# Retention attention with a routed expert layer on one core: loads in halves, and the first and last steps in another order

## The chip, the cores and the metric

The kernel runs on one core of one Trainium2 chip. A core has five engines that run their own instruction lists beside each other: TensorE (PE, matmuls), VectorE (DVE), ScalarE (ACT), GpSimd (POOL) and SyncE (SP, which here issues most of the transfers between memory and the core). They wait for each other only by semaphores. The core's 16 DMA engines move the data. The metric is device time in microseconds (us) of the core, from launch to end; lower is better.

## The reference

Attention here is a retention recurrence without softmax: per head a state of 64 x 64 decays by gamma and takes in k v^T, and the query reads it. Its result, 3072 tokens of 512 features, goes to a layer of 4 groups of 4 experts; each token takes the best group and in it the best expert, and its row is scaled by the product of both softmax weights.

```python
# q, k, v: (4, 8, 768, 64)   batch, heads, tokens, head size
gamma = 1 - 2 ** (-5 - arange(8));  scale = 1 / sqrt(64)
for t in range(768):
    state = gamma * state + k[:, :, t] (x) v[:, :, t]
    y[:, :, t] = scale * q[:, :, t] @ state
x = y as (3072, 512)
g = argmax(x @ w_group);  e = argmax(x @ w_expert[g])
out[token] = g_weight * e_weight * relu(x @ w1[g, e]) @ w2[g, e]   # 512 -> 1024 -> 512
```

## The kernel before

**Attention.** The 768 tokens of a sequence are 6 chunks of 128. A step takes one chunk of two sequences, so there are 12 steps (NS2 = 12; step i is chunk i % 6). A chunk is computed with full matrices: scores of its own 128 tokens (`score_mm`), masked to the lower triangle on DVE (`score_mask`, pf), times the values (`value_out`), plus the state of the chunks before times the queries (`state_out`), both added in PSUM (op). The values are scaled beforehand by a power of gamma on POOL (`vprep`, vs). `keys_mm` transposes the keys on PE and ACT copies them (kk); `state_mm` adds kk x vs to the state, and ACT copies it (V). `out_x` multiplies op by the decay table gx on DVE: xt, the step's output. One step later xt gives the router's logits (`logits_mm`, ACT copies them to ls) and is transposed to rows of tokens (`trans_mm`, ACT copies them to xr), which SP writes to the scratch tensor xd; four small matmuls in `trans_mm` (L326, the selections) bring the logits to a token per partition in the bank log.

**Routing.** Per two steps one batch of 512 tokens is routed (`route`): on DVE max, exp (ACT), group and expert hits (oh, L374); on PE the ranks of the tokens within their experts (L399, L401); on DVE the slot numbers (slot, L419) and the weights (six small operations, L382 to L394, which end in src). POOL then scatters (token, weight) by slot into the lists `meta` in memory, four scatters per batch (`enlist`, L440).

**Experts.** Experts 0 and 1 are computed in two parts: ua, va with the tokens of the first 12 chunks, which start while attention still runs, and ub, vb with the rest. The 14 others follow in order of their counts, as us[0] to us[13] (`order` sorts on DVE). An expert needs its weights (wf, four tiles of 1 MB, which SP loads), split into a high half in f16 (wh, ACT, L616) and a low half in bf16 (wl = wf - wh, DVE, L618); its list (mt, SP, L630) and the rows of its tokens by an indirect gather on POOL (xg, L640); their transposes (tpx, PE) split into xbh (ACT) and xbl (DVE, L661). A product is three matmuls of halves: hps = xbh wh + xbl wh + xbh wl (L681), its positive part goes to hh (ACT) and hl (DVE, L689), and the second product yps follows alike (L713). The result is weighted on ACT and scattered by POOL to the output (L814).

**Order.** No scheduler sets it: each engine runs its instructions in the order in which the Python code writes them. `attention` writes the steps; its callback `beside(i, place)` puts the early experts' work between them, and `extra` the early splits on POOL and ACT. `run` then writes the passage to the experts by hand: `first(n)` takes n half pieces of ua's first product, of which there are eight, and `route` is a generator that gives way at "wait" and "ranks". `self.held` collects the hl operations of this passage, to be written later.

**Banks.** PSUM has eight banks: sh0 to sh2 (tag "big", also the hidden products), sh3 (tag "tra"), op (two, "mid"), log, and "sta" (state, later free). The scores of the first sequence go to sh0 and sh1, of the second to sh2 and sh3; logits, transposes and key transposes share them. Who writes a bank next waits for its last reader.

**Transfers.** SP issues the loads in the order of the code: at the start first q, k of step 0 by halves, the constants `cst` (571 columns, 285.5 KB) between them, then the other loads of steps 0 to 2 and the decay table. A q, k or v of a step is one transfer of 128 x 1024 (512 KB), and so is kt for two steps and the write of xr.

## Time and profile before

| | us |
|---|---|
| median of three runs | 427.3 (426.33 to 429.1) |
| the profiled execution, its own time | 427.34 |
| its span in the trace | 425.6 |
| PE busy | 404.0 (95%) |
| DVE busy | 290.1 (68%) |
| ACT busy | 222.8 (52%) |
| POOL busy | 175.9 (41%) |

Times within the trace count from the start of the span. Attention fills the first 107 us, the passage to the experts ends near 135 us, and the experts take the rest. A row of the timeline gives the start, the length, the engine, the line, what is written and read, and in brackets how long the engine had been idle before and what ended that. Rows that follow each other are put together (x32); of such a row the bracket is that of the first. PE's matmuls are pipelined, so a row's length holds the end of its last matmul, and the next row can start within it. The profile's granted clock is a share of full speed, 2.4 GHz.

### The profile page before, as it was taken

The numbers are of one execution on the slowest core, as the hardware profiler recorded it, in microseconds if no ns is written. First come the engines' busy times: TensorE is split into PE (matmuls) and PEld (weight loads), VectorE is DVE, ScalarE is ACT, GpSimd is POOL, SyncE is SP. The second block draws the span as 40 slices with busy tenths as digits, with TensorE's granted clock in tenths as the row PEclk, the third lists the DMA queues.
The fourth block names the chain that finished last, engine by engine and source line by source line (L and its number), as shares of the span: only waits on it lengthen the run. The fifth ranks groups of instructions, "written<-read, shape, count | busy, mean of one in ns | idle before, by whom it ended". The sixth has DMA issues, their size and how long they took to land.

```text
span 425.6 us, 13495 instructions
## 1 busy us (share of the span) xinstructions
PE 404.0 (95%) x5692; PEld 332.4 (78%) x5721; DVE 290.1 (68%) x473; ACT 222.8 (52%) x342; POOL 175.9 (41%) x153
## 2 busy tenths in 40 slices
PE   8899999999798999999999999999999999999991
PEld 4789888787675768585979788897978878879791
DVE  4455585578892557776889786867768777787620
ACT  2135336446541556646556665665766657667520
POOL 4445669748877022340508142351513405222001
PEclk9999999999999999999999999999999999999996
DMA  8999999997536867776776786978788797896001
GB/s 282 378 313 327 373 306 339 336 285 243 161 94 236 333 220 249 245 258 235 257 246 214 259 277 239 315 246 283 266 286 284 272 306 270 280 327 233 27 9 34
DMA packets 36913, 107.94 MB, mean 254 GB/s; under 512 B 13784, under 2 KB 13784, under 8 KB 29684
## 3 DMA queue, kind: packets, MB, share of 16 engines
q1 hardware_dynamic: 25908, 89.76, 61.9%
q0 software_dynamic: 10944, 17.31, 11.7%
q8 instruction: 45, 0.74, 0.7%
q14 instruction: 16, 0.13, 0.1%
HBM read 94.65 MB, written 13.77 MB: 255 GB/s over the span
## 4 chain that ended last, share of the span: by engine, by line
PE 58%; issue 26%; POOL 6%; DMA 4%; DVE 2%; SPq 1%; ACT 0%; POOLq 0%; DVEq 0%; ACTq 0%
PE hps L681 19%; PE yps L713 8%; PE yps L759 6%; PE yps L761 5%; PE op L291 5%; POOL out L814 4%; PE sh L227 3%; POOL xg L640 2%; PE op L278 2%; DMA gx<-dec 2%; PE sh L322 2%; PE tpx L658 2%; PE stp L253 2%; PE sh L310 2%; PE sh L212 1%
## 5 line engine op out<-in xcount | busy, mean ns | idle before, releaser
L618 DVE TENSOR_TENSOR wl<-wf,wh 128x1024 bf16<-128x1024 f32 x120 | 148.5, 1248 | 40.0 <-ACT wh L616 35.4
L681 PE MATMUL hps<-xbh,wh 128*128 128x128 f16 (+14 forms) x576 | 134.2, 245 | 0.9 <-ACT xr L329 0.9
L681 PE MATMUL hps<-xbl,wh 128*128 128x128 bf16 (+14 forms) x576 | 134.2, 245 | 0.3 <-issue 0.3
L616 ACT ACTIVATE wh<-wf 128x1024 f16<-128x1024 f32 (+1 forms) x136 | 133.5, 1002 | 1.8 <-DMA wf<-w1p 1.8
L681 PE MATMUL hps<-xbh,wl 128*128 128x128 f16 (+14 forms) x576 | 134.2, 245 | 0.1
L814 POOL DMA_INDIRECT out<-yo,mt x32 | 41.3, 1289 | 180.4 <-ACT yo L796 152.7
L681 PEld LDWEIGHTS <-wh 128*128 128x128 f16 x1152 | 102.5, 98 | 4.7 <-issue 1.9
L640 POOL DMA_INDIRECT xg<-xd,mt x32 | 52.5, 1641 | 26.3 <-DMA mt<-meta 17.4
L686 ACT ACTIVATE hh<-hps 128x256 f16<-128x256 f32 (+14 forms) x72 | 35.1, 488 | 52.3 <-PE hps L681 51.5
L761 PEld LDWEIGHTS <-wh 128*128 128x128 f16 x704 | 44.7, 98 | 21.0
L681 PEld LDWEIGHTS <-wl 128*128 128x128 bf16 x576 | 56.3, 98 | 1.1 <-issue 0.5
L239 DVE TENSOR_TENSOR pf<-sh,cst 128x512 f32<-128x512 f32 x48 | 30.8, 685 | 30.0 <-PE sh L227 10.3
L689 DVE SCALAR_TENSOR_TENSOR hl<-hps,hh 128x256 bf16<-128x256 f32 (+14 forms) x69 | 38.1, 553 | 16.7 <-ACT hh L686 14.2
L660 ACT ACTIVATE xbh<-tpx 128x512 f16<-128x512 f32 (+13 forms) x32 | 16.9, 527 | 47.2 <-PE tpx L658 47.1
L661 DVE TENSOR_TENSOR xbl<-tpx,xbh 128x512 bf16<-128x512 f32 (+13 forms) x32 | 19.2, 601 | 21.5 <-ACT xbh L660 21.5
L440 POOL DMA_INDIRECT meta<-src,slot x24 | 27.6, 1151 | 14.3 <-DVE src L394 7.1
L759 PE MATMUL yps<-wh,hh 128*128 128x512 f16 x88 | 33.4, 380 | 0.0
L759 PE MATMUL yps<-wh,hl 128*128 128x512 f16 x88 | 33.4, 379 | 0.0
L187 POOL TENSOR_TENSOR vs<-lv,cst 128x512 f32<-128x512 f32 x24 | 24.6, 1047 | 20.8 <-DMA lv<-qkv 10.9
L761 PEld LDWEIGHTS <-wl 128*128 128x128 bf16 x352 | 23.1, 98 | 10.4
L761 PE MATMUL yps<-hh,wl 128*128 128x103 f16 (+10 forms) x352 | 26.3, 197 | 1.2
L761 PE MATMUL yps<-hl,wh 128*128 128x103 bf16 (+10 forms) x352 | 26.3, 197 | 0.0
(146 smaller groups left out, 600.0 us busy)
## 6 DMA issues: line engine op xcount, KB each, us to landing
wf<-w1p SPq DMA_DIRECT2D x26, 1024.0 KB
wf<-w2p SPq DMA_DIRECT2D x26, 1024.0 KB
xd<-xr SPq DMA_DIRECT2D x12, 512.0 KB
lq<-qkv SPq DMA_DIRECT2D x11, 512.0 KB
lk<-qkv SPq DMA_DIRECT2D x11, 512.0 KB
lv<-qkv SPq DMA_DIRECT2D x11, 512.0 KB
wf<-w1p SPq DMA_DIRECT2D x16, 256.0 KB
wf<-w2p SPq DMA_DIRECT2D x16, 256.0 KB
```

What stands on the lines that cost most here:

```text
L239: nc.vector.tensor_tensor(o, sc, tri, ALU.mult)
L440: i = nc.gpsimd.indirect_dma_start(out=self.metaf, out_offset=bass.IndirectOffsetOnAxis(ap=slot[:, c:c + 1], axis=0), in_=src[:, c, :], in ...
L616: nc.scalar.activation(u["wh"][i][:, cs], u["wf"][i][:, cs], AF.Copy)
L618: (eng or nc.vector).tensor_tensor(u["wl"][i][:, cs], u["wf"][i][:, cs], u["wh"][i][:, cs], ALU.subtract)
L640: nc.gpsimd.indirect_dma_start(out=xg[0:r, i, :], out_offset=None, in_=self.xd[0:n, :], in_offset=bass.IndirectOffsetOnAxis(ap=mt[0:r, i, ...
L681: nc.tensor.matmul(hv[:, a, 0:W], l[:, k, fs], r[:, k, 0:W], start=(n == 0), stop=(n == 11))
L686: nc.scalar.activation(hh[:, f, 0:W], hv[:, :, 0:W], AF.Relu)
L689: nc.vector.scalar_tensor_tensor(*rest)
L713: nc.tensor.matmul(ps[0:r, :], l[:, k, ts], m[k], start=(n == 0), stop=(n == 23))
L759: nc.tensor.matmul(big, h[:, k, 0:P], w[k], start=(n == 0), stop=(n == 23))
L761: nc.tensor.matmul(yv[:, d, 0:r], w[k][:, d * P:d * P + P], h[:, k, P:P + r], start=(n == 0 and d == 0), stop=(n == 23), skip_group_check= ...
L814: s = nc.gpsimd.indirect_dma_start(out=self.out, out_offset=bass.IndirectOffsetOnAxis(ap=mt[0:r, i, 0:1].bitcast(U32), axis=0), in_=yo[0:r ...
```

## The change

It has eight parts, none of which alters what is computed.

1. Loads of q, k, v, kt and the writes of xr go in two transfers of 256 KB each.
2. The constants are two tiles: `cst` (308 columns, 154 KB, what the first steps use) keeps its place, `rest` (263 columns) comes last in the front's order. That order puts the decay table ahead of v1, q2 and k2. The cast of `stri` moves to the end of step 1.
3. In steps 0 and 1 the scores of the next step are written behind `out_x` (in step 1 they stood around `state_out`), so xt stands ahead of the masks. The key transposes of steps 1 and 2 use log and sh0.
4. Selections of steps 4, 8, 9 and 10 are postponed into the next step (`late`, `select_late`).
5. In the last two batches the weights are written directly behind the hits, not behind the slots.
6. The low splits (wl) of va move behind the slots, the held hl and xbl of va; the high splits (wh) are dealt anew over the last step and the passage. `xlow(ua)` stands behind the last xt.
7. The last step's logits have a bank of their own (tag "sta"), its xr a buffer of its own; the fourth hidden product of ua and va uses "tra", the other three "big". The transposes of the last step stand ahead of all hidden products. ACT clears the buffer xg1 in place of POOL.
8. The gathers of ub and vb stand directly behind the last scatters on POOL. At step 10 POOL's scaling `vprep` stands ahead of the gathers of ua and va. Two in place of four weight parts go ahead of the early lists on SP.

Here is SP's row of transfers at the start, in the kernel before (lq, lk, lv are the loads, a number more is another tile, gx the decay table):

```order
L122 DMA cst_93<-cst 128x571
L177 DMA lq_94<-qkv 128x512
L177 DMA lk_96<-qkv 128x512
L177 DMA lv_150<-qkv 128x512 x2
L177 DMA lq_153<-qkv 128x1024
L177 DMA lk_155<-qkv 128x1024
L177 DMA lq_157<-qkv 128x1024
L177 DMA lk_159<-qkv 128x1024
L177 DMA lv_161<-qkv 128x1024
L190 DMA gx_116<-dec 128x512
L879 DMA wr_114<-wr 128x4x20
```

And with the change:

```order
L125 DMA cst_93<-cst 128x308
L179 DMA lq_95<-qkv 128x512
L179 DMA lk_97<-qkv 128x512
L179 DMA lv_150<-qkv 128x512 x2
L179 DMA lq_153<-qkv 128x512 x2
L179 DMA lk_156<-qkv 128x512 x2
L192 DMA gx_117<-dec 128x512
L179 DMA lv_160<-qkv 128x512 x2
L179 DMA lq_163<-qkv 128x512 x2
L179 DMA lk_166<-qkv 128x512 x2
L908 DMA wr_115<-wr 128x4x20
L906 DMA rest_94<-cst 128x263
```

The decay table stands three loads of a whole step further ahead, and the tile of the constants ahead of the second q and k is smaller.

DVE in the last step and the passage, before, from the hits of the fifth batch (oh) to the first row of the sixth:

```order
L374 TENSOR_TENSOR oh<-log,go 128x64
L661 TENSOR_TENSOR xbl<-tpx,xbh 128x4x128
L303 TENSOR_TENSOR xt<-op,gx 128x512 x2
L407 TENSOR_TENSOR log<-log,nb 128x64
L410 TENSOR_TENSOR nb<-log,nb 128x16
...
L419 CAST slot<-log 128x4
L382 TENSOR_REDUCE log<-ex 128x20
...
L394 RECIPROCAL src_127<-log 128x4
L618 TENSOR_TENSOR wl<-wf,wh 128x1024 x3
L689 SCALAR_TENSOR_TENSOR hl<-hps,hh 128x2x128
L358 TENSOR_REDUCE m<-log 128x20
```

With the change, the same stretch:

```order
L391 TENSOR_TENSOR oh<-log,go 128x64
L399 TENSOR_REDUCE log<-ex 128x20
...
L411 RECIPROCAL src_127<-log 128x4
L306 TENSOR_TENSOR xt<-op,gx 128x512 x2
L687 TENSOR_TENSOR xbl<-tpx,xbh 128x4x128
L426 TENSOR_TENSOR log<-log,nb 128x64
...
L438 CAST slot<-log 128x4
L375 TENSOR_REDUCE m<-log 128x20
```

and further on, behind the sixth batch's slots, where the splits now stand:

```order
L438 CAST slot<-log 128x4
L449 TENSOR_SCALAR rows_2187<-nb 1x1
L449 TENSOR_SCALAR rows_2189<-nb 1x1
L1117 SCALAR_TENSOR_TENSOR hl<-hps,hh 128x2x128 x4
L687 TENSOR_TENSOR xbl<-tpx,xbh 128x4x128
L637 TENSOR_TENSOR wl<-wf,wh 128x1024 x4
L480 TENSOR_TENSOR cnt<-nb,rest 1x16
```

The weights have moved ahead of the last xt, and three splits that stood between the fifth batch's weights and the sixth batch's hits now stand, with a fourth, behind the sixth batch's slots and ahead of the list that `order` makes.

POOL in the passage, before, from the last early split to the gathers of ub and vb:

```order
L618 TENSOR_TENSOR wl<-wf,wh 128x512
L1054 MEMSET xg_1973 128x1024
L440 DMA meta<-src_129,slot 57600x2 x4
L594 TENSOR_LOAD ord
L814 DMA out<-yo,mt 3072x512
L640 DMA xg_80<-xd,mt 128x512 x2
L590 ISA
```

With the change:

```order
L637 TENSOR_TENSOR wl<-wf,wh 128x512
L459 DMA meta<-src_129,slot 57600x2 x4
L659 DMA xg_80<-xd,mt 128x512 x2
L613 TENSOR_LOAD ord
L841 DMA out<-yo,mt 3072x512
L609 ISA
```

The clearing is gone from POOL, and the two gathers stand ahead of the read of the sorted order and of ua's output.

The diff, cut to its core:

```diff
@@ load
-        n, f = "qkv".index(name), slice(us[0] * DM, us[-1] * DM + DM)
-        self.nc.sync.dma_start(st[name].rearrange("p u f -> p (u f)")[:, f], self.a_qkv[n, i][:, f])
+        for u in us:
+            self.nc.sync.dma_start(st[name][:, u], self.a_qkv["qkv".index(name), i][:, u * DM:u * DM + DM])
@@ logits_mm
-        lt = self.sh[bank][:, 0:2 * P]
+        lt = self.pp.tile([P, 512], F32, name="lgt", tag="sta", bufs=1) if bank is None else self.sh[bank]
+        lt = lt[:, 0:2 * P]
@@ trans_mm
-        xr = self.wp.tile([P, 2, DM], F32, name="xr", bufs=1)
+        if not late:
+            self.select_mm(i)
+        xr = (pool or self.wp).tile([P, 2, DM], F32, name="xr", bufs=1)
...
@@ route
-        last = c0 + n == NCH
+        soon = c0 + n >= NCH - BM
...
+        if soon:
+            yield from weights()
         yield "wait"
...
-        if not last:
+        if not soon:
             yield "wait"
-        yield from weights()
+            yield from weights()
@@ layers
-            ps = pp.tile([P, 512], F32, name="hps", tag="big", bufs=3)
+            tag = u.get("banks", ["big"] * 4)[f2]
+            ps = pp.tile([P, 512], F32, name="hps", tag=tag, bufs=3 if tag == "big" else 1)
@@ attention
-        for o in "qB0 kB0 vA0 vB0 q1 k1 q2 k2 v1 d0 w0".split():
+        for o in "qB0 kB0 vA0 vB0 q1 k1 d0 v1 q2 k2 w0 c0".split():
...
-                scores(i + 1, 0)
+                if i > 1:
+                    scores(i + 1, 0)
+                if not last:
+                    self.select_late()
                 if i % 2 == 0:
                     self.route_steps(99, True)
                 self.state_out(i, 0)
+                self.select_late()
                 self.state_out(i, 1)
-                scores(i + 1, 1)
+                if i > 1:
+                    scores(i + 1, 1)
...
-            if i == 0:
-                scores(1, 0)
-                scores(1, 1)
             self.out_x(i)
+            if i < 2:
+                scores(i + 1, 0)
+                scores(i + 1, 1)
...
-                self.keys_mm(i + 1)
+                self.keys_mm(i + 1, banks=(self.log, self.sh[0]) if i < 2 else None)
@@ beside, place 0 and 2
                     if i == 10:
                         self.wsplit(va, 0, low=False)
-                        self.wsplit(va, 1, low=False)
-                    if last:
-                        self.wsplit(va, 0, high=False)
...
-                        self.xtrans(ua, 'big', (0,))
-                        self.wsplit(va, 2, low=False)
+                        self.xtrans(ua, 'big', (0,), low=False)
+                        self.wsplit(va, 1, low=False)
@@ run, the passage
-            nc.gpsimd.memset(self.xg[1], 0.0)
...
-            self.logits_mm(last, 3)
-            for k in (1, 2, 3):
-                self.wsplit(va, k, high=False)
-            first(2)
-            self.trans_mm(last)
+            self.logits_mm(last)
+            self.trans_mm(last, self.yp)
...
-            self.wsplit(va, 4, low=False)
-            self.wsplit(va, 5, low=False)
             self.held = []
             first(4)
+            self.wsplit(va, 3, low=False)
             next(route)
-            first(2)
+            first(4)
...
-            self.xtrans(va)
+            self.xtrans(va, "sta")
+            for k in range(2):
+                nc.scalar.activation(self.xg[1][:, k], self.one, AF.Copy, scale=0.0)
+            self.wsplit(va, 4, low=False)
+            self.wsplit(va, 5, low=False)
             self.listed(ub)
             self.listed(vb)
+            self.gather(ub)
+            self.gather(vb)
+            for k in range(4):
+                self.wsplit(va, k, high=False)
             self.steps.append(self.order())
             self.route_steps(99)
-            self.wsplit(va, 4, high=False)
-            self.wsplit(va, 5, high=False)
...
-            self.gather(ub)
-            self.gather(vb)
...
             for i, k in enumerate(self.layers(va)):
-                if i in (1, 3):
-                    self.wsplit(va, 6 + i // 2)
+                if i in (1, 3, 5, 7):
+                    k = 4 + i // 2
+                    if k < 6:
+                        self.wsplit(va, k + 2, low=False)
+                    self.wsplit(va, k, high=False)
```

## Rows read from the trace of the kernel before

**Rows 1.** The page: the span, and each engine's busy time and instructions.

```profile
span 425.6 us, 13495 instructions
...
PE 404.0 (95%) x5692; PEld 332.4 (78%) x5721; DVE 290.1 (68%) x473; ACT 222.8 (52%) x342; POOL 175.9 (41%) x153
```

**Rows 2.** Stretches: from:to, length, busy us (instructions) by engine, clock, DMA share, GB/s.

```profile
12.00:18.00 6.00, 4.91 (x122) 3.67 (x117) 3.75 (x7) 1.74 (x3) 2.00 (x2) 1.00 1.05 396
...
70.00:100.00 30.00, 28.59 (x618) 24.22 (x613) 22.06 (x63) 12.99 (x27) 19.71 (x20) 1.00 0.95 311
...
110.00:120.00 10.00, 7.73 (x98) 6.26 (x98) 8.78 (x28) 4.74 (x9) 8.78 (x7) 1.00 0.53 150
```

**Rows 3.** The chain of waits at the start: start, us, what.

```profile
2.73 4.92 DMA lk<-qkv
...
7.67 9.03 DMA gx<-dec
```

**Rows 4.** Timeline of DVE, start: start, us, instruction, idle before and its end.

```profile
6.34 0.23 DVE L136 CAST stri<-cst 128x128 bf16<-128x128 f32 x1 [2.82 <-DMA cst<-cst]
...
16.73 1.29 DVE L303 TENSOR_TENSOR xt<-op,gx 128x512 f32<-128x512 f32 x2 [0.92 <-DMA gx<-dec]
```

**Rows 5.** Timeline of PE in the first steps.

```profile
15.47 1.44 PE L227 MATMUL sh<-lq,lk 64*64 64x128 f32 x32
...
18.16 0.99 PE L278 MATMUL op<-lq,V 64*64 64x128 f32 x27 [0.20 <-DVE xt L303]
...
25.51 0.90 PE L227 MATMUL sh<-lq,lk 64*64 64x128 f32 x32
```

**Rows 6.** Timeline of PE in the passage to the experts.

```profile
107.35 0.64 PE L310 MATMUL sh<-xt,wr 128*32 128x256 f32 x8 [0.97 <-ACT xr L329]
...
112.91 0.22 PE L681 MATMUL hps<-xbh,wh 128*128 128x128 f16 x1 [0.90 <-ACT xr L329]
...
115.73 0.20 PE L399 MATMUL log<-oh,stri 128*128 128x80 bf16 x1 [1.32 <-DVE oh L374]
...
117.65 0.38 PE L713 MATMUL yps<-wh,hh 128*128 128x512 f16 x1
...
132.53 0.66 PE L658 MATMUL tpx<-ident,xg 128*128 128x128 f32 x4 [1.58 <-DMA xg<-xd,mt]
```

**Rows 7.** Timeline of ACT in the passage.

```profile
112.27 1.08 ACT L329 ACTIVATE xr<-sh 128x512 f32<-128x512 f32 x2 [2.41 <-DMA xd<-xr]
...
123.09 0.69 ACT L796 ACTIVATE yo<-yps,mt 128x512 f32<-128x512 f32 x1 [4.64 <-PE yps L713]
```

**Rows 8.** Timeline of DVE in the last step and the passage: low splits.

```profile
98.36 3.39 DVE L618 TENSOR_TENSOR wl<-wf,wh 128x1024 bf16<-128x1024 f32 x1
...
108.68 4.61 DVE L618 TENSOR_TENSOR wl<-wf,wh 128x1024 bf16<-128x1024 f32 x3
...
122.83 2.35 DVE L618 TENSOR_TENSOR wl<-wf,wh 128x1024 bf16<-128x1024 f32 x2
```

**Rows 9.** Timeline of POOL from step 10 to the gather of ub.

```profile
96.17 1.08 POOL L640 DMA_INDIRECT xg<-xd,mt  x1 [6.63 <-DMA mt<-meta]
...
98.62 2.05 POOL L187 TENSOR_TENSOR vs<-lv,cst 128x512 f32<-128x512 f32 x2
...
112.19 1.95 POOL L440 DMA_INDIRECT meta<-src,slot  x1 [0.30 <-PE hps L681]
...
117.83 0.97 POOL L1054 MEMSET xg<- 128x1024 f32 x1
118.97 1.00 POOL L440 DMA_INDIRECT meta<-src,slot  x1 [0.17 <-DVE hl L1081]
...
122.98 1.93 POOL L440 DMA_INDIRECT meta<-src,slot  x1 [0.30 <-DVE ord L490]
...
129.08 1.05 POOL L640 DMA_INDIRECT xg<-xd,mt  x1 [2.88 <-DMA mt<-meta]
```

**Rows 10.** Timeline of SP: the list reads.

```profile
126.08 3.94 SPq L630 DMA_DIRECT2D mt<-meta  x5
```

More of the change, by code (lines that the diff above doesn't have):

```diff
@@ L109, in __init__ @@
         self.held = None
+        self.late = None
         self.waiting = False
@@ L315, in logits_mm, with select_mm, select_late, trans_mm @@
         nc.scalar.activation(s["ls"], lt, AF.Copy)
-    def trans_mm(self, i):
+    def select_mm(self, i):
+        nc, s = self.nc, self.st[i]
+        for u in range(2):
+            a = LG + 20 * (i % 2 * 2 + u)
+            lg = self.log[:, a:a + 20]
+            nc.tensor.matmul(lg, s["ls"][:, u * P:u * P + P], self.rest[:, C_SEL:C_SEL + 20], start=True, stop=True)
+    def select_late(self):
+        if self.late is not None:
+            self.select_mm(self.late)
+            del self.st[self.late]
+            self.late = None
+    def trans_mm(self, i, pool=None, late=False):
         nc, s = self.nc, self.st[i]
@@ L322, in trans_mm @@
                 nc.tensor.transpose(self.sh[2 + u][:, j * P:j * P + P], s["xt"][:, j, u], self.ident)
-        for u in range(2):
-            a = LG + 20 * (i % 2 * 2 + u)
-            lg = self.log[:, a:a + 20]
-            nc.tensor.matmul(lg, s["ls"][:, u * P:u * P + P], self.cst[:, C_SEL:C_SEL + 20], start=True, stop=True)
-        xr = self.wp.tile([P, 2, DM], F32, name="xr", bufs=1)
+        if not late:
+            self.select_mm(i)
+        xr = (pool or self.wp).tile([P, 2, DM], F32, name="xr", bufs=1)
         for u in range(2):
@@ L330, in trans_mm @@
         g, c = divmod(i, NC)
-        xd = self.xd.rearrange("(b r) f -> r b f", r=S)[c * P:c * P + P, 2 * g:2 * g + 2, :]
-        nc.sync.dma_start(xd, xr)
+        for u in range(2):
+            row = (2 * g + u) * S + c * P
+            nc.sync.dma_start(self.xd[row:row + P, :], xr[:, u])
     def route(self, i):
@@ L660, in xtrans, with xlow @@
             nc.scalar.activation(xh[:, :, ts], tv[:, :, 0:r], AF.Copy)
-            nc.vector.tensor_tensor(xl[:, :, ts], tv[:, :, 0:r], xh[:, :, ts], ALU.subtract)
+            u["tv", i] = tv
+            if low:
+                self.xlow(u, i)
+    def xlow(self, u, i):
+        r = u["rows"][i]
+        ts = slice(i * P, i * P + r)
+        self.nc.vector.tensor_tensor(u["xl"][:, :, ts], u["tv", i][:, :, 0:r], u["xh"][:, :, ts], ALU.subtract)
     def layers(self, u):
@@ L1017, in beside @@
                 last = i == NS2 - 1
+                for k in range(*NEXT.get((i, place), (0,))):
+                    self.wload_part(va, k)
                 if place == -1 and i == 10:
@@ L1042, in beside @@
                     if last:
-                        self.wsplit(va, 3, low=False)
+                        self.xlow(ua, 0)
+                if place == 3:
+                    if last:
+                        self.wsplit(va, 2, low=False)
             self.wp = pool("wp", 2)
```

65 lines of the change are left out of this document (37 added, 28 removed).

## The prediction

> **What bounds the kernel now.** I read the page first. The span is 425.6 us and TensorE (PE) is busy in 404.0 of them [rows 1]; the granted clock is 1.00, the 2.4 GHz level, in each stretch below [rows 2], so a higher clock can give nothing back. The change adds no matmul and takes none away. What can be won is therefore idle time of PE, some 21 us, and only where it lies. The busy time by stretch [rows 2] shows the places: in 12 to 18 us PE works 4.91 of 6.00, in 110 to 120 us only 7.73 of 10.00, while in 70 to 100 it works 28.59 of 30.00. The DMA engines are full at the start (share 1.05 at 396 GB/s) and nearly full in 70 to 100 (0.95), but half idle in 110 to 120.
>
> The chain of waits says why PE idles at the start: two transfers are links of it, the second half of the first keys, landed at 7.65, and the decay table gx, landed at 16.70 [rows 3]. VectorE (DVE) waits for gx with the first xt [rows 4], and PE for that xt [rows 5]. For the passage from attention to the experts I read PE's waits [rows 6]; the rows of the engines that they name [rows 7 to 9] say why those were late.
>
> **The start: constants, order of loads, scores.** The constants sent ahead shrink from 285.5 to 154 KB; 131.5 KB fewer go ahead of the second half of the first step. Between the two landings [rows 3] came 4637.5 − 1309.5 = 3328 KB in 9.05 us, 368 KB/us. So what hangs on the first loads, up to the scores of step 1, comes 0.36 us sooner. Behind the first keys now stand the first values (two pieces of 256 KB), the halves of q1 and k1 (four) and gx (one): seven pieces, 1792 KB or 4.87 us. gx lands at 7.65 − 0.36 + 4.87 = 12.2 in place of 16.70. The first xt (1.29 [rows 4]) is then done by 13.5, before PE is through with the scores and key transposes of step 1, and it stands ahead of the masks on DVE, which hold it up no more.
>
> Before, PE began half of step 2's scores at 15.47 and got going in state_out at 18.16 [rows 5]. Of these 2.69 us the 32 scores took 0.90 (the same 32 in the row at 25.51) and two state_out matmuls some 0.06: 1.73 idle, all of it behind xt. In the new order nothing there needs xt. What is late next: value_out needs v1, which lands at 13.6, and behind it at most two scalings on GpSimd (POOL), 2.05 for the pair [rows 9], which makes 15.6; PE is there at about 15.5. The scores of step 2, now behind the logits, need q2 and k2, 1536 KB behind gx, at 16.4, and PE comes there near 19. I take 0.2 for new small waits. **Start: 1.73 + 0.36 − 0.2 = 1.9 us.** Ends: 2.2, and nothing if the data of later steps bound it (first rival).
>
> **Halves of 256 KB.** The bound from below is a row: the constants landed at 6.32 (DVE's cast waited for them [rows 4]) and two pieces of 256 KB behind them at 7.65 [rows 3], 385 KB/us, not less than the 368 of the transfers of 512 KB. I cost the cut at nothing while transfers queue. The bound from above is that the start's gain is given back. The Trainium skill, "DMA: Bandwidth & Descriptors", section Bandwidth, speaks against the cut: batch transfers to 1 MiB or more for 75% of the peak. By the curve in "SBUF — State Buffer" (the Trainium skill), section The DMA setup-cost knee, a transfer of 256 KiB by itself reaches 224 GB/s; at that rate attention would lose far more than the change can win. The row of 385 speaks against that for transfers in a queue.
>
> **Selections.** They are four small matmuls each. All but one of the postponed ones still share a bank with the scores ahead of them and wait as before: nothing.
>
> **Passage to the experts.** Three waits stand before PE is at the first expert's second product, at 117.65 [rows 6]: 0.97 (the last step's logits wait for ScalarE (ACT) to empty bank sh3), 0.90 (the third hidden bank is one that ACT still reads; ACT itself had waited 2.41 for the transfer of the xr before [rows 7]) and 1.32 (ranks wait for DVE's hits, late behind three splits of 4.61 [rows 8]). Sum 3.19.
> The change gives the logits a bank of their own, the last xr a buffer of its own, takes the third hidden bank elsewhere, and puts the splits behind the slots. All three causes go. New waits: xt of the last step now stands behind six weight operations that stood behind the slots before, and the last select may find its copy behind a weight split on ACT; I allow 0.2 for both together. **Passage: 3.19 − 0.2 = 3.0**; ends 2.5, if each costs double, and 3.4, if the restarts behind three waits go too.
>
> What is late next is DVE. It begins the four splits of the second expert about 1 us (the last held low part and one xbl) behind the second product's start, 117.65 − 3.0 = 114.65 (times in before's clock), at 115.6. At 1.18 each, as the pair at 122.83 [rows 8], they end at 120.3. The second product lasts from 117.65 to its result at 123.09 [rows 6, 7], 5.4, so PE comes to the second expert at 120.1, needs the second split at about 120.4 and the last two from 122.8. The cover holds with 2 us to spare.
>
> **Gathers.** PE loses 1.58 at 132.53 waiting for the gather of the third list [rows 6]. The chain: the last scatter into the lists ends at 124.91 [rows 9], the list is read from 126.08 [rows 10], the gather starts at 129.08 after 2.88 of waiting [rows 9], its data are there at 132.53: 7.6 us from the scatter's end. POOL's scatters come sooner now: a scaling of 2.05 goes into the 6.63 that POOL idled before, a clearing of 0.97 has gone, and two scatters that were stretched beside DVE's splits (one of them the 1.95 at 112.19) take 1.00, as the one at 118.97 [rows 9], so 1.8 less. The last four start 4.8 sooner, at 114.2. With their gaps of 0.3 they take 5.2, and the data come 5.4 sooner, at 127.1; or three of them lie beside the new splits at 1.93, as the one at 122.98 [rows 9], and the data come 2.6 sooner, at 129.9. PE comes 3.0 sooner than 130.95, at 127.95. The stall becomes 0 to 2.0; I leave it as it was and count nothing. ACT clears the second gather buffer in place of POOL, while PE is in the second product: nothing. The first dynamic expert's weights are issued 2 us or more sooner while PE is 3.0 sooner, and are used a whole expert later: nothing. From there it is one expert after another with PE full; what is won before is kept.
>
> **Sum.** 1.9 + 3.0 = 4.9. The profiled execution took 427.34, as the median of the runs, 427.3: **422.4 us**. A measurement of this kernel tells about 1%, 4.3 us, from no change, so faster means at most 423.0.
>
> **Rivals.**
> *The transfers hold attention (0.22).* Where a later step waits for its data, two microseconds won at the start are waited out there. For it: the DMA share of 0.95 in 70 to 100, where PE idles 1.4 of 30 [rows 2]. Against: the order only moves bytes, and 131.5 KB leave the front. Then 427.34 − 3.0 = 424.3; were the halves dearer by 2 to 5% (33 loads of q, k and v of 512 KB are 46 us at 368 KB/us), 1 to 2 more, 425 to 426.5. The skill's rule on batching would show so.
> *The gathers catch up (0.15).* With the scatters unstretched the stall of 1.58 goes too: 420.9.
> *Splits and POOL collide (0.08, slower).* The split at 98.36 took 3.39 beside POOL's scaling at 98.62 [rows 8, 9], against 1.18. The new run of four lies beside the last scatters. Beginning at 115.6, it makes the second expert's third hidden product wait as soon as a split takes more than about 1.8 (four by 122.8). At 3.39 the four end at 129.2: 6.4 lost; the order list and four more splits follow on DVE, and two of these beyond the 1.18 are another 2 × 2.2 late, of which PE's remaining hidden product hides some 2. Gain 4.9 less 8.8: 431. For it: the collision is in the trace. Against: three splits at 108.68 beside two scatters averaged 1.54 [rows 8]. The Trainium skill, "SBUF — State Buffer", section Who interferes with whom, says that a DVE operation with two SBUF inputs contends with a GpSimd operation that reads SBUF, and only infers that such an operation leaves descriptor generation alone; the trace agrees on the scaling, while scatters of 1.93 and 1.95 against 1.00 elsewhere leave the second open.
> *The change does less than it says (0.05).* Another engine is late at the same three places: 425 to 428.
>
> **Numbers.** The forecast holds 0.50, its own range 421 to 424.5. A little over two thirds of it lies at 423.0 or below, 0.36; with the gathers 0.51 faster. Within 1%: the rest of the forecast, 0.14, most of the transfers, 0.20, and of the last rival, 0.04: 0.38. Slower: 0.11, the collision's 0.08 and 0.03 for dearer halves with other waits. The range leaves out the collision, the dearest halves and what is below the gathers' case: 419.8 to 426.8.
>
> **What the new profile would show.** Start: gx landed near 12.2, no wait for xt, the scores of step 3 near 23.6 in place of 25.51. Transfers: PE above 28.5 of 30 in 70 to 100 us; a wait for lq, lk or kk there would mean the first rival. Passage: no wait of PE above 0.4 before the first expert's second product, which starts near 112.8; splits of at most 1.6 behind it. Gathers: a wait for xg of 0 to 2.0. I am wrong if PE waits for wl (collision), or if the steps between 25 and 100 us take longer than before by what the start won.

## The result: 422.5 us in place of 427.6, and the profile after

Six runs of each kernel gave a median of 422.51 us (420.29 to 425.09) for the change and 427.61 (426.33 to 429.24) before, a ratio of 0.9891 (95% interval 0.9856 to 0.9926). The forecast of 422.4 is met in the sum. It is not met in the terms: they erred against each other, so that the sum came out is in part luck. In what follows the ratios are of the fast executions of each kernel, while the traces of e3, e5_early and e6 are of slower executions, so that sizes read from these three do not stand for the ratios beside them.

The profiled execution of the changed kernel is its fastest run, 420.29; its span is 7.0 us shorter than that of before, where the medians differ by 5.1. The page's lines that answer to [rows 1], with the transfers that carry instructions:

```profile
span 418.6 us, 13575 instructions
...
PE 401.2 (96%) x5692; PEld 331.5 (79%) x5721; DVE 287.2 (69%) x473; ACT 225.0 (54%) x344; POOL 172.2 (41%) x152
...
q8 instruction: 45, 0.74, 0.7%
```

The stretches of [rows 2], now:

```profile
12.00:18.00 6.00, 5.74 (x146) 4.96 (x144) 3.68 (x6) 1.68 (x3) 3.05 (x3) 1.00 1.07 370
...
70.00:100.00 30.00, 26.87 (x609) 23.86 (x606) 19.36 (x60) 14.33 (x29) 22.60 (x22) 1.00 1.01 304
...
110.00:120.00 10.00, 9.38 (x98) 6.60 (x99) 8.27 (x21) 6.04 (x10) 5.88 (x6) 1.00 0.39 107
```

PE's idle time in 12 to 18 and in 110 to 120 us has mostly gone (0.26 and 0.62 us are left of 1.09 and 2.27), as forecast, but in 70 to 100 it idles 3.1 us where it idled 1.4, and where the prediction wanted less than 1.5. The start, on DVE (the row that answers to [rows 4]) and on PE:

```profile
12.45 1.29 DVE L306 TENSOR_TENSOR xt<-op,gx 128x512 f32<-128x512 f32 x2 [2.37 <-DMA gx<-dec]
```

```profile
15.56 1.10 PE L281 MATMUL op<-lq,V 64*64 64x128 f32 x31 [0.26 <-issue]
...
21.02 1.10 PE L230 MATMUL sh<-lq,lk 64*64 64x128 f32 x40 [0.26 <-issue]
...
23.53 1.26 PE L340 MATMUL sh<-ident,xt 128*128 128x128 f32 x8 [0.38 <-DVE pf L242]
...
25.07 0.90 PE L230 MATMUL sh<-lq,lk 64*64 64x128 f32 x32
```

DVE's wait for gx ends at 12.45, and no matmul waits for xt. Yet step 3's scores begin at 25.07, only 0.44 sooner than in [rows 5], where the prediction wanted 23.6. Attention's end and the passage on PE, beside [rows 6]:

```profile
79.07 0.80 PE L256 MATMUL stp<-vs,kk 128*64 128x64 f32 x20 [2.00 <-issue]
...
91.22 0.62 PE L327 MATMUL log<-rest,ls 128*128 128x20 f32 x4 [1.02 <-DVE slot L438]
...
106.38 0.62 PE L327 MATMUL log<-rest,ls 128*128 128x20 f32 x4 [0.51 <-ACT ls L319]
...
110.56 0.20 PE L418 MATMUL log<-oh,stri 128*128 128x80 bf16 x1 [0.87 <-DVE src L411]
...
113.82 0.38 PE L740 MATMUL yps<-wh,hh 128*128 128x512 f16 x1
...
126.95 0.60 PE L677 MATMUL tpx<-ident,xg 128*128 128x128 f32 x4
```

The three waits of 3.19 are gone; two new ones of 0.51 and 0.87 stand there, against the prediction's sign that none would be above 0.4, and the third list's transposes wait for nothing. To see where the time went I set the same five places of PE's list side by side (starts in us). a0 is a second profile of the unedited changed kernel and b0 a second one of the kernel before, both on chip 1.

| PE begins | before | b0 | changed | a0 | won since the line above against before, changed / a0 | the same against b0 |
|---|---|---|---|---|---|---|
| value matmuls of step 2 | 28.03 | 30.40 | 27.44 | 26.71 | 0.59 / 1.32 | 2.96 / 3.69 |
| value matmuls of step 11 | 102.33 | 107.40 | 100.23 | 101.26 | 1.51 / -0.25 | 4.21 / 2.45 |
| transposes of the second list | 117.21 | 121.48 | 113.38 | 114.28 | 1.73 / 1.86 | 0.93 / 1.06 |
| transposes of the third list | 132.53 | 136.60 | 126.95 | 128.51 | 1.75 / 1.09 | 1.55 / 0.89 |
| transposes of the first dynamic expert | 154.03 | 157.32 | 147.62 | 149.21 | 0.83 / 0.80 | 0.05 / 0.02 |
| end of the span | 425.6 | 428.3 | 418.6 | 420.2 | 0.59 / 0.58 | 0.00 / -0.01 |

Up to step 11 the two profiles of the kernel before lie further apart (2.4 and 2.7 us) than the change was to win there, so one pair of profiles sizes the terms there to no better than about 2 us, and those behind to about 1.

### The profile page after: what moved, and what is told of

Its sections match the earlier page's. It is cut to its first block, busy times and chain, and to the rows that moved or that the text cites. A ratio compares the mean times of both kernels' runs of the same rounds, so it can differ in the third digit from the quotient of the medians.

```text
span 418.6 us, 13575 instructions
## 1 busy us (share of the span) xinstructions
PE 401.2 (96%) x5692; PEld 331.5 (79%) x5721; DVE 287.2 (69%) x473; ACT 225.0 (54%) x344; POOL 172.2 (41%) x152
## 4 chain that ended last, share of the span: by engine, by line
PE 60%; issue 22%; POOL 7%; DMA 5%; SPq 1%; DVE 1%; ACT 0%; POOLq 0%; ACTq 0%; DVEq 0%
PE hps L708 21%; PE yps L740 10%; PE yps L786 6%; PE yps L788 5%; PE op L294 4%; POOL out L841 4%; PE sh L230 3%; POOL xg L659 3%; DMA wf<-w2p 3%; PE tpx L677 2%; PE stp L256 2%; PE sh L340 2%; PE op L281 2%; PE sh L215 1%; DMA wf<-w1p 1%
## 5 line engine op out<-in xcount | busy, mean ns | idle before, releaser
L637 DVE TENSOR_TENSOR wl<-wf,wh 128x1024 bf16<-128x1024 f32 x120 | 145.1, 1219 | 39.8 <-ACT wh L635 39.6
L189 POOL TENSOR_TENSOR vs<-lv,cst 128x512 f32<-128x512 f32 x24 | 24.6, 1046 | 20.1 <-DMA lv<-qkv 12.2
L687 DVE TENSOR_TENSOR xbl<-tpx,xbh 128x512 bf16<-128x512 f32 (+13 forms) x32 | 19.2, 601 | 17.2 <-ACT xbh L679 17.1
L459 POOL DMA_INDIRECT meta<-src,slot x24 | 24.2, 1009 | 14.8 <-DMA lk<-qkv 6.2
```

The source lines that it names most:

```text
L189: self.nc.gpsimd.tensor_tensor(o, v, g, ALU.mult)
L637: (eng or nc.vector).tensor_tensor(u["wl"][i][:, cs], u["wf"][i][:, cs], u["wh"][i][:, cs], ALU.subtract)
```

## The experiments

The experiments ran on three chips, on each beside the kernel before. On chip 1 the changed kernel's own ratio was 0.989 again. On chips 13 and 14 every kernel made from it came out at 1.003 or above: in all eight traces it is 19.2 to 22.7 us from the value matmuls of step 9 to those of step 11, in the changed kernel and a0 15.75 and 15.85. The kernel before had medians of 429.3 and 429.8 us on these two chips, at most 2.2 above the 427.6 of the result. So I compare times only within a chip, and read each edit's effect from its own place in the trace.

**The changed kernel again (a0, chip 1) and the kernel before (b0, chip 1).** No edit.

> The changed kernel itself, unedited, beside the kernel before on the chip of this call, since four single edits of it all ran at 1.00 to 1.02 of the kernel before on another chip, and all four traces lose 6 to 8 us between the value matmuls of step 9 and those of step 11 (PE pauses by 0.6 us with the wait put down to issue, from 94 to 101 us, and then runs at a granted clock of 0.50 for 3.4 to 6.8 us). Theory A, the loss belongs to that chip and not to the edits: on a chip that does it, this run shows it too and the ratio to the kernel before is 1.00 to 1.01; on a chip that doesn't, the ratio is 0.989 and PE is not paused. Theory B, the four edits each brought it: no pauses here, ratio 0.985 to 0.993 on any chip.

> The kernel before, unedited, for its trace on the same chip. If the pauses of PE in 94 to 101 us belong to a chip, they stand here too, at the same place, and the span is 428 to 432; if they belong to the change (its gathers, its transfers), this trace has no stretch between 90 and 112 us at a granted clock below 1.00 and lies within 1 us of the earlier trace at step 11 (102.3).

a0: 424.35, ratio 0.9892 (0.9805 to 0.9979), no pauses. That alone fits both of its theories. What decides is the edits: in e3, e4 and e6 below, all five engines' lists are the changed kernel's until past the place where PE pauses, so these edits did not bring the loss, and a0 shows that the change does not bring it everywhere. b0: one run, 430.01, no pauses either, but it meets neither half of its expectation: step 11 stands at 107.40 and not within 1 us of 102.3. It has waits for issue of 1.32, 1.65 and 1.45 at 70, 79 and 85 us, one of 2.46 for the keys at 102, and this one at the start, behind which the granted clock is 0.50, the 1.2 GHz level, from 19.3 to 22.7 us:

```profile
18.47 0.40 PE L278 MATMUL op<-lq,V 64*64 64x128 f32 x2 [1.58 <-DVE xt L303]
```

In e3's trace PE looks so at the pauses (first its timeline, then its stretches, and those of a0):

```profile
98.77 0.36 PE L256 MATMUL stp<-vs,kk 128*64 128x64 f32 x4 [0.32 <-issue]
99.53 0.36 PE L256 MATMUL stp<-vs,kk 128*64 128x64 f32 x5 [0.40 <-issue]
100.28 0.36 PE L256 MATMUL stp<-vs,kk 128*64 128x64 f32 x5 [0.40 <-issue]
```

```profile
94.00:101.00 7.00, 5.52 (x116) 4.62 (x115) 2.55 (x9) 1.08 (x2) 4.17 (x5) 1.00 0.90 300
101.00:106.00 5.00, 4.29 (x48) 3.13 (x48) 1.99 (x4) 1.99 (x4) 4.33 (x4) 0.66 0.51 181
```

```profile
94.00:101.00 7.00, 7.00 (x145) 5.89 (x135) 3.39 (x9) 3.31 (x7) 5.80 (x6) 1.00 1.00 341
101.00:106.00 5.00, 5.00 (x70) 3.81 (x69) 4.52 (x18) 3.02 (x7) 3.77 (x4) 1.00 1.02 257
```

Every 0.75 us PE does a handful of matmuls and stops. Behind the pauses the granted clock is at the 1.2 GHz level from 101.9 to 105.3 us (0.66 on the mean of 101 to 106), and a0 has neither; e5_splits has the pauses too and keeps 1.00. Neither the changed kernel as it is nor a profile of the kernel before was taken on chips 13 and 14. So what makes PE pause stays open, and that the change wins anything there is not shown: e3, e4 and e6, the changed kernel itself up to step 11, take 20.7 to 22.7 us from step 9 to step 11, where the kernel before took 16.2 and 17.5 in its two traces.

**Whole transfers (e1, chip 14).**

```diff
-        for u in us:
-            self.nc.sync.dma_start(st[name][:, u], ...)
+        self.nc.sync.dma_start(st[name].rearrange("p u f -> p (u f)")[:, f], self.a_qkv[n, i][:, f])
```

The two other transfers that part 1 cut, the keys and xr, are whole again in the same way.

> The changed kernel with whole transfers of 512 KB for a step's q, k, v, kt and the write of xr; everything else as changed, the order of the front too. Theory A, the halves cost nothing while transfers queue: the time stays with the changed kernel's 422.5 within 1 us, step 3's scores start near 25.1 as with the halves, and the DMA share in 70 to 100 us stays near 1.0. Rival B, the halves are dearer (the share rose from 0.95 to 1.01 at fewer GB/s): the share falls back to 0.95 at 310 GB/s, the front lands gx earlier than 12.4, and the kernel is 1 to 2 us faster than the changed one, 420.5 to 421.5. Rival C, halves help, since consumers start on the first: 1 us or more slower, 423.5 or above.

Ratio 1.0036 (1.0007 to 1.0064), against 1.0033 (0.9992 to 1.0074) for e3 with halves on the same chip. gx has landed by 12.52 and step 3's scores begin at 24.95, with halves at 12.45 and 25.07. Stretches of e1, then of e3 (DMA share and GB/s stand last):

```profile
24.00:50.00 26.00, 26.00 (x614) 23.70 (x617) 15.80 (x39) 11.45 (x23) 14.23 (x15) 1.00 0.98 337
```

```profile
24.00:50.00 26.00, 25.20 (x600) 22.84 (x600) 15.26 (x38) 9.25 (x21) 13.58 (x14) 1.00 1.02 350
```

A GB/s costs the same share in both (0.98 / 337 and 1.02 / 350 are 0.0029). Theory A: the cut costs nothing and wins nothing that this shows; the two intervals leave room for about 1.5 us either way, and e3 has an edit of its own.

**Step 2's scores back around the state matmuls (e2, chip 14).**

```diff
-            if i < 2:
+            if i < 1:
                 scores(i + 1, 0)
...
-                if i > 1:
-                    scores(i + 1, 0)
+                scores(i + 1, 0)
...
-                if i > 1:
-                    scores(i + 1, 1)
+                scores(i + 1, 1)
...
-                self.keys_mm(i + 1, banks=(self.log, self.sh[0]) if i < 2 else None)
+                self.keys_mm(i + 1, banks=(self.log, self.sh[0]) if i < 1 else None)
```

> The changed kernel with step 2's scores back around the state matmuls of step 1 (and the key transposes of step 2 in the banks of before); the decay table stays early, so xt still comes ahead. Theory A, the start's gain was lost to new waits that this part made (the transposes behind the logits waited 0.54 for the masks of the scores put right ahead of them): step 3's scores start 0.5 to 1.0 sooner than 25.07, near 24.3, and the kernel is as much faster, near 421.8. Rival B, the start is bound by what the transfers deliver or by PE's own restarts (gaps of 0.5 that name no other engine): step 3's scores stay at 25.1 within 0.2 and the time at 422.5 within 0.5. Rival C, this part was the start's gain: step 3's scores at 25.5 or later.

Step 3's scores at 25.86, later than 25.07 and than the 24.26 to 24.97 of the three other kernels on this chip: theory A falls. Ratio 1.0086 (1.0057 to 1.0115). Two other waits took the place of the one for the masks:

```profile
14.77 0.66 PE L215 MATMUL sh<-ident,lk 128*128 128x128 f32 x4 [0.84 <-DVE pf L242]
16.36 0.90 PE L230 MATMUL sh<-lq,lk 64*64 64x128 f32 x31 [0.94 <-ACT kk L216]
```

The edit keeps step 1's key transposes in the new banks, so it does not return to the start of before; with a wait of 1.25 for issue in the same start, it does not tell the rivals B and C apart.

**The loads' order of before (e8, chip 13).**

```diff
-        for o in "qB0 kB0 vA0 vB0 q1 k1 d0 v1 q2 k2 w0 c0".split():
+        for o in "qB0 kB0 vA0 vB0 q1 k1 q2 k2 v1 d0 w0 c0".split():
```

> The changed kernel with the loads of the start in the order of before (q2, k2 and v1 ahead of the decay table; the small tile of the constants and the halves stay). Theory A: the table's place is the start's gain: gx lands 4 us later than 12.4, xt and the logits of step 1 wait for it, the scores of step 2 behind them too, and step 3's scores start 2 to 3 us later than the changed kernel's 24.3 to 25.1; the ratio is 0.994 to 0.996. Rival B, attention is bound by its transfers all along: the 2 to 3 us are made up by step 8, and the ratio is 0.989. Rival C: step 3's scores start at the same time within 0.5.

Ratio 1.0178 (1.0135 to 1.0221). DVE's first xt and what PE waits for:

```profile
17.40 1.29 DVE L306 TENSOR_TENSOR xt<-op,gx 128x512 f32<-128x512 f32 x2 [7.75 <-DMA gx<-dec]
```

```profile
19.34 1.12 PE L215 MATMUL sh<-ident,lk 128*128 128x128 f32 x4 [5.19 <-DVE pf L242]
...
22.31 3.36 PE L294 MATMUL op<-pf,vs 128*64 128x128 f32 x32
```

Theory A in kind, at more than twice the size: step 3's scores begin at 31.62, in the other three kernels on the chip at 24.06 to 24.83. Since xt now stands ahead of the masks, a late table blocks them too, and behind the wait of 5.19 the granted clock is at the 1.2 GHz level from 18.4 to 25.2. Step 2's value matmuls begin at 33.99, in the other three at 26.44 to 27.88; at step 9 it is 91.87 against 85.00 to 87.23. Of a delay of 6.1 to 7.6 us, 4.6 to 6.9 is still there. So attention's transfers take back little of what the start loses: rival B, my first rival, does not hold here.

**No postponed selections (e9, chip 1).**

```diff
-                late = i + 1 in KEYED or i % NC == NC - 2
+                late = False
```

> The changed kernel with no selection postponed. In the changed trace the postponed selection of step 8 waited 1.02 for a slot operation of DVE in the same bank, where the kernel before waited 0.21 and 0.45 at that step. Theory A, postponing costs more there than it wins: without it the waits at steps 4, 8, 9 and 10 are 0.2 to 0.4 each for the copy of the logits, the wait of 1.02 goes, and the kernel is 0.3 to 0.8 faster than the unedited changed one. Rival B, it wins 0.2 to 0.4 at each of the four: 0.5 to 1 slower without it. Both are near what five comparisons can tell; the trace decides.

422.80, ratio 0.9855 (0.9764 to 0.9945) against a0's 0.9892. The wait of 1.02 is gone, and none of the four selections waits 0.4. The times lie on theory A's side but inside each other's intervals. It reaches the third list sooner than its data:

```profile
128.29 0.63 PE L677 MATMUL tpx<-ident,xg 128*128 128x128 f32 x4 [1.91 <-DMA xg<-xd,mt]
```

**The early half of part 8 undone (e5_early, chip 1).**

```diff
-NEXT = {(9, 0): (0, 2), (9, 3): (2, 4), (10, 0): (4, 8), (11, 0): (8, 12)}
+NEXT = {(9, 0): (0, 4), (10, 0): (4, 8), (11, 0): (8, 12)}
...
+            beside(i, -1)
             if not last:
                 self.vprep(i + 1)
-            beside(i, -1)
```

> The changed kernel with part 8's early half undone: four weight parts ahead of the early lists on SP, and the gathers of ua and va ahead of POOL's scaling in step 10. Theory A, that half is worth nothing by itself while PE is busy: as the unedited changed kernel of this call within 1 us. Rival B, the gathers that now run beside the fullest transfers make the pauses of PE in 94 to 101 us: without them no pauses, 5 us or more faster than the unedited changed kernel wherever that one shows them. Rival C, the early scatters behind it are what let the third list's data come in time: PE waits 1 us or more for xg and the kernel is as much slower.

Ratio 0.9879 (0.979 to 0.9968), as a0: theory A by the times. Its trace, of an execution of 430.02, has waits of 2.92 for the keys and of 3.40 for the third list, so rival C is not excluded; rival B can't show itself where the unedited kernel has no pauses.

**The sixth batch's weights behind its slots (e3, chip 14), and with two more edits (c2, chip 13).**

```diff
-        soon = c0 + n >= NCH - BM
+        soon = c0 + n == NCH - BM
```

c2 has this line and two more:

```diff
-                late = i + 1 in KEYED or i % NC == NC - 2
+                late = False
...
-                if place == 3:
-                    if last:
-                        self.wsplit(va, 2, low=False)
...
             self.trans_mm(last, self.yp)
+            self.wsplit(va, 2, low=False)
```

> The changed kernel with the weights of the sixth batch behind its slots again (those of the fifth stay behind their hits). Theory A: the ranks waited 0.87 in the changed kernel for the last weight operation, which reads and writes the same bank log, though they need only the hits; without the weights ahead the ranks come 0.9 to 1.1 sooner, no wait of PE above 0.2 stands there, the first expert's second product starts 0.9 sooner, and the kernel takes about 421.6. Rival B, the wait has another cause (an ACT operation or PE's own order): the wait stays and so does the time. Rival C, what is won is lost behind it, since the weights now push the held low parts and the splits by 0.3 to 1.2: second product 0.9 sooner, a new wait for xbl or wl of 0.5 or more, time 422.5.

> A version meant to beat both: the changed kernel with three edits, each against a wait seen in its traces. No selection postponed (a wait of 1.25 at step 9 for slot operations in the same bank); the sixth batch's weights behind its slots (ranks waited 1.0 for the weights, and not at all in the single edit's trace); the high split of va's third part behind the last step's xr on ACT (the last selection waited 0.55 to 0.67 for its logits' copy behind it). Theory A: the three waits shrink to 0.4 or less each, 1.5 to 2.3 us against the changed kernel, a ratio to the kernel before of 0.984 to 0.987. Rival B: what is won ends in the next wait (the third list's data, which PE then reaches 1.5 sooner): the wait for xg grows by as much and the ratio stays at 0.989.

Ratios 1.0033 and 1.005 (1.0021 to 1.0079): c2 does not beat the kernel before, and neither comparison can show 1 us beside the pauses. The wait can be read all the same: the ranks stand without a wait in both traces, in e3 at

```profile
116.90 0.20 PE L418 MATMUL log<-oh,stri 128*128 128x80 bf16 x1
```

In the changed kernel, a0, e9 and e1 alike, they waited 0.87 for the last weight. DVE there, with the splits that follow:

```profile
109.23 0.24 DVE L399 TENSOR_REDUCE log<-ex 128x20 f32<-128x80 f32 x1
...
110.33 0.18 DVE L411 RECIPROCAL src<-log 128x4 f32<-128x4 f32 x1
...
115.26 4.62 DVE L637 TENSOR_TENSOR wl<-wf,wh 128x1024 bf16<-128x1024 f32 x4
```

The hits were ready at 109.2, the ranks began at 110.56: theory A for the wait. That it carries to the second product is not shown: in e3 it begins 12.28 us behind the logits of step 10, in e1 on the same chip 12.43, in the changed kernel 11.69. And e3's trace has the collision that the prediction feared, with the roles changed: a scatter that lies beside the four splits of DVE (these take 4.61, as the 4.62 above) is stretched, and PE waits for the third list:

```profile
124.47 4.54 POOL L459 DMA_INDIRECT meta<-src,slot  x1 [0.30 <-issue]
...
138.70 0.63 PE L677 MATMUL tpx<-ident,xg 128*128 128x128 f32 x4 [3.41 <-DMA xg<-xd,mt]
```

c2 has the first line of e3 too, and there the scatter beside the splits took 1.33 and PE did not wait. c2 was to show that three such edits add up; on chip 13 it shows no gain.

**Logits and xr as before (e6, chip 13).**

```diff
-            self.logits_mm(last)
-            self.trans_mm(last, self.yp)
+            self.logits_mm(last, 3)
+            self.trans_mm(last)
```

> The changed kernel with the last step's logits in bank sh3 and its xr in the buffer of the steps before, as in the kernel before; the rest of the passage as changed. Theory A: both waits of the kernel before come back, 0.97 before the logits and, behind the transfer of the xr before, up to 0.9 at the hidden product that takes a bank of the transposes; part of it overlaps the wait for the ranks (1.0): the first expert's second product 1 to 1.9 later than in the changed kernel against step 11, the ratio 0.991 to 0.994. Rival B: the hits and the ranks' wait hide all of it: ratio as changed, 0.989.

Ratio 1.0124 (1.006 to 1.0189), 0.7% above c2 and 0.9% above e5_splits on the same chip, though the three intervals overlap. ACT and PE:

```profile
118.18 1.09 ACT L345 ACTIVATE xr<-sh 128x512 f32<-128x512 f32 x2 [3.50 <-DMA xd<-xr]
```

```profile
122.06 0.23 PE L418 MATMUL log<-oh,stri 128*128 128x80 bf16 x1 [3.62 <-DVE src L411]
```

The xr that waits for a transfer holds ACT, behind it the exponential of the hits, and so the ranks: from the logits of step 10 to the ranks 11.12 us, in the changed kernel 8.43. Theory A in kind, by this one trace 2.7 in place of at most 1.9. The logits' bank alone was 0.43, and the wait for the third hidden bank did not come back.

**Low splits at the places of before (e5_splits, chip 13).**

```diff
+                    if last:
+                        self.wsplit(va, 0, high=False)
...
             self.logits_mm(last)
+            for k in (1, 2):
+                self.wsplit(va, k, high=False)
...
-            for k in range(4):
-                self.wsplit(va, k, high=False)
+            self.wsplit(va, 3, high=False)
```

> The changed kernel with the low splits of va's first three parts at the places of before on DVE: one in step 11, two between the last xt's followers and the sixth batch's hits. Theory A: the one in step 11 falls into 2 us in which DVE waits anyway, and the two in the passage push the hits by 1.2, since DVE idled 1.7 there: ranks and second product 1.0 to 1.5 later than in the changed kernel, ratio 0.992. Rival B: the hits are not what PE waits for there (the weights behind them are): under 0.5. Rival C: a split beside POOL's scaling takes 3.4 again and pushes the fifth batch too: 2 us or more.

Ratio 1.0037 (1.0007 to 1.0066), as c2 on the same chip. DVE and PE:

```profile
110.19 2.36 DVE L637 TENSOR_TENSOR wl<-wf,wh 128x1024 bf16<-128x1024 f32 x2
```

```profile
115.98 0.20 PE L418 MATMUL log<-oh,stri 128*128 128x80 bf16 x1 [1.87 <-DVE log L409]
```

The ranks wait 1.0 more, 9.19 from the logits of step 10 in place of 8.43: theory A, 0.8 to 1.0.

**The gathers at the old place (e4, chip 14).**

```diff
-            self.gather(ub)
-            self.gather(vb)
             for k in range(4):
                 self.wsplit(va, k, high=False)
...
             for k in self.first:
                 pass
+            self.gather(ub)
+            self.gather(vb)
```

> The changed kernel with the gathers of ub and vb behind the read of the sorted order and ua's output again. Theory A, the place of the gathers on POOL took the wait of 1.58 for the third list away: the sorted order is ready at 122.7, the output takes 1.4, so the gather starts 2 to 2.6 later than 122.7, its data are there near 128.6, PE waits 1.5 to 2 for them and the kernel is 1.5 slower than the changed one, near 424. Rival B, the earlier scatters alone did it (they end 5.5 sooner, beside no split): the wait stays below 0.4, and the time at 422.5 within 0.5.

Ratio 1.0166 (1.0117 to 1.0215), 1.3% above e1 and e3, 5.6 us where 1.5 was expected. POOL and PE, and POOL of the changed kernel:

```profile
125.57 0.98 POOL L459 DMA_INDIRECT meta<-src,slot  x1 [0.30 <-issue]
...
136.80 1.06 POOL L659 DMA_INDIRECT xg<-xd,mt  x1 [0.30 <-issue]
```

```profile
140.36 0.63 PE L677 MATMUL tpx<-ident,xg 128*128 128x128 f32 x4 [2.17 <-DMA xg<-xd,mt]
```

```profile
116.06 1.27 POOL L459 DMA_INDIRECT meta<-src,slot  x1 [0.30 <-issue]
...
122.71 1.05 POOL L659 DMA_INDIRECT xg<-xd,mt  x1 [5.38 <-DMA mt<-meta]
```

From the last scatter's end to the gather it is 10.2 us at the old place and 5.4 at the new one (4.3 to 7.2 over all traces with the new place); PE waits 2.17 here, and not for this list in e1 and e2 on the same chip. Theory A for the gather's place; e3, with the new place, waits longer, for the scatter shown above, and the rest of the 5.6 us has no cause shown.

## Why the sum was right and the terms were not

**The start: 1.9 forecast, 0.6 and 1.3 measured against one profile of the kernel before, 3.0 and 3.7 against the other.** The table's place was right (gx there by 12.45 for 12.2; e8 shows that the new order of scores needs it). The ten traces with this start have step 3's scores at 24.06 to 25.07, the two of the kernel before at 25.51 and 28.02; the later one has the wait of 1.58 for xt and the stretch at 1.2 GHz behind it. So 1.9 lies within what the traces show, and the forecast 23.6 does not. The term that failed for certain is "I take 0.2 for new small waits". The transposes behind the logits wait for the masks of scores put right ahead of them (0.38, and 0.37 to 0.39 in every trace that keeps them there), and in the changed kernel two waits for issue of 0.26 with their restarts stand in the same stretch. The 0.36 of the smaller constants can't be seen: the first value matmuls start at 9.55, before at 9.53, and over the twelve traces with the small tile anywhere from 8.81 to 10.15.

**Halves: right**, as far as e1 can tell: the same share for a GB/s, and times that differ by less than their intervals. The Trainium skill's rule on batching ("DMA: Bandwidth & Descriptors", section Bandwidth) does not show here, for transfers in a full queue.

**Selections: nothing forecast, a wait of 1.02 found.** "Wait as before" overlooked that the postponed selection writes the bank in which DVE works on a batch at that step; before, 0.21 and 0.45 stood there, and e9 has the 1.02 no more.

**Passage: 3.0 forecast, 1.7 and 1.9 measured, 0.9 and 1.1 against b0.** All three waits went, also by b0, which has 0.97, 1.01 and 0.41 there. e6 brings back the one for the logits' bank (0.43) and a longer one for the ranks through ACT, e5_splits lengthens that for the ranks by 1.0; the third hidden bank was not tested by itself. The mis-sized term is "0.2 for both together". The select's wait for its copy, which I had named, measured 0.51. The other, 0.87, I had not: I had counted the moved weights as a delay of xt, which nobody felt, but the sixth batch's weights stand in the same bank ahead of the ranks, which therefore wait for them; in e3 and c2, where they stand behind, the wait is gone. (3.19 less 0.51 and 0.87 is 1.81. The lower end of the forecast, "2.5, if each costs double", was added up wrongly: doubling the 0.2 gives 2.8.)

**DVE's cover: right** here, four splits in 4.62 and no wait for wl; the collision stayed away from the splits. It is thinner than I had it: e1, e2, e6 and e8 show waits of PE for wl of 0.87 to 1.24 behind it, and e3's scatter of 4.54 shows the collision on POOL's side.

**Gathers: nothing forecast, 1.75 and 1.1 measured, 1.55 and 0.9 against b0.** The wait is 0 and 0.49, in the range that I left open and near my second rival: in these two traces the scatters of the passage went at 0.97 to 1.27. But it is 1.91 in e9 and 3.41 in e3, so part of this is luck.

**The rest of attention: nothing forecast, +1.5 and -0.25, +4.2 and +2.5 against b0.** The two profiles of the changed kernel differ there by 1.8, those of the kernel before by 2.7, for the most part in the steps that have waits for issue, which the last section tells of, or in b0 the wait of 2.46 for the keys. What of the difference is the change's stays open.

**Behind the passage: nothing forecast, 0.83 and 0.59.** b0 takes 20.72 and 270.98 us for these two stretches, as the changed kernel and a0 do (20.67 and 270.98, 20.70 and 270.99). So these 1.4 us belong to the one profile of the kernel before, and are not the change's.

By the first pair of profiles errors of -1.3 and -1.3 in the start and the passage stand against +1.5, +1.75 and +1.4, which makes 7.0, since the profiled run of the changed kernel is its fastest. The medians say 5.1 for a forecast of 4.9. The mechanism is shown where a wait was named and went (xt, the three of the passage); how near the sum came is in part luck.

## What to carry to other kernels

Where an operation is moved ahead, look at the bank it writes: here a matmul that shares the bank waited for it (0.87, 1.02) though it needed none of its result, and so a move that delays nobody by its length can still add a wait. A forecast by waits removed should price a new wait for every neighbour that becomes adjacent, at the size of the old ones and not at a tenth. And a sum that fits proves no term: compare stage by stage, and look at a second profile of both kernels before giving a microsecond a cause. The second profile of the kernel before took 1.4 us away from the change that one pair had given it.

## What the runs showed of the hardware

PE can wait for its own instructions. The trace has 45 instruction transfers of 16 KB for PE's 11,413 instructions, 254 to each. From 12 to 94 us the fourteen traces hold 30 waits of PE above 0.4 us put down to issue (up to 2.00, as that at 79.07), one to four in each, and counted in PE's list every one stands at the same place in a run of 256 instructions, at the 193rd or 194th. The transfers' own records settle what it waits for: each of the 30 waits ended 0.8 to 1.6 us after the end of an instruction transfer (that at 79.07 after one that ran from 76.64 to 77.57), and at the same place of all 191 runs in this stretch PE never went on sooner than 0.7 us after one. From 150 to 400 us, where that transfer had ended at least 5.4 us ahead, none of 315 such places has a wait. The run of 256 that holds the wait at 79.07 has it in ten of the fourteen traces; the others change from trace to trace. Such waits stand in the steps in which two profiles of one kernel part: a0 is 1.85, 0.68 and -0.89 us behind the changed kernel in three steps, and within 0.1 in the six others from step 2 to step 11.

Why the transfer comes late there is not shown. From 12 to 94 us the DMA engines are full (share 1.01, against 0.74 from 150 to 400), but PE also goes through 256 instructions in 6.0 us, against 11.1; no run separates the two.

The pauses between 95 and 106 us in all eight traces of chips 13 and 14 are another thing: they come every 0.75 us, not at that place, and I don't know their cause.

A scatter of POOL can be stretched by a low split of DVE (wl) beside it. Over the fourteen traces the 309 scatters that overlap no split took 0.97 to 1.12 us each; of the 27 that overlap one, 15 took 1.14 to 4.54. The four splits in a row took 4.61 beside the scatter of 4.54 and 4.62 beside that of 1.27, so here the splits did not give way.

A list was read 1.2 to 4.6 us after the last scatter into it had ended, which moves the third list's data by more than the 1.58 of the whole term.
